# The spectrum of a filter layer kept in the four column groups of its first stage, with GpSimd and VectorE doing the reordering

## The chip, the cores and the metric

One core of one Trainium2 chip. The time is that of the device for one execution, in microseconds (us), as a median of several executions. Besides the times, each kernel was run once with the hardware profiler, whose page and trace are quoted. In these, PE is TensorE's matmuls, PEld its weight loads, ACT is ScalarE, DVE is VectorE, POOL is GpSimd and SP the engine that issues most loads.

## The reference

Two branches on the same input x (2048 rows of 1024 bf16), mixed by a gate, and the gradient of the whole:

```python
def _A_ref(x, w_r, w_i):                      # spectral branch
    X = rfft2(x.astype(float32))              # 2048 x 513 complex
    X = X * (w_r + 1j * w_i)                  # filters, 2048 x 513 each
    return irfft2(X, s=(S, D)).astype(bfloat16)

def _B_ref(x, w1, b1, w2, b2):                # MLP branch, F = 3584
    h = x @ w1 + b1
    h = where(h > 0, h, 0); h = h * h
    return h @ w2 + b2

g = sigmoid((x * gate_w).sum(-1, keepdims=True))
out = g * _A_ref(x, ...) + (1 - g) * _B_ref(x, ...)
# returned: out, and the gradients of x, w_r, w_i, w1, b1, w2, b2, gate_w for grad_out
```

The spectral branch runs forward (on x) and backward (on the gradient) at once; the filters' gradients are products of the two spectra.

## The kernel before

The transform has three parts. A first stage makes, for each row tile, the column transform in four groups of columns (column number modulo 4) and stores it. A middle stage, 16 values of m, finishes the row transform, multiplies by the filters and goes back. A last stage reloads and inverts the columns. The middle stage runs as a generator interleaved with the weight-gradient products of the MLP (chains of 16 matmuls 128x512, accumulated in a bank pw and copied out as wo), a share of steps of the transform per chain. The framework has a scheduler of its own: within these priorities it fixes the order of instructions on each engine.

Parts that the change touches (cuts are marked):

```python
def transform(m, n, pm, x):                   # middle stage: px, then x
    px = fps.tile([P, 2, H], FP32, ..., tag="ps2", bufs=2)      # H = 512
    for T in range(2):
        mm(px[:, T, :], lhsT=am[:, m, n, :], rhs=pm[:, n, T, :], ...)
    for c in range(2):
        nc.scalar.copy(                       # from groups to natural order
            out=x[lanes[n], c, :, 0:H].rearrange("p t (i g) -> p t g i", g=4),
            in_=px[lanes[c]].rearrange("p t (g i) -> p t g i", g=4))

def grads_of_w(m, x):                         # filter gradients
    # ... t1_, t2_: products of the two spectra, on VectorE
    V(out=gs[:, 0, 0:W1], in0=t1_[:, 0, 0:W1], in1=t1_[:, 1, 0:W1], op=ALU.add)
    V(out=gs[:, 1, 0:W1], in0=t2_[:, 1, 0:W1], in1=t2_[:, 0, 0:W1], op=ALU.subtract)
    nc.scalar.mul(out=gw[:, :, 0:W1], in_=gs[:, :, 0:W1], mul=GS)
    # ... edges halved on VectorE, gw stored

for m in range(NM + 1):                       # NM = 16; yields left out
    # transform(m, 0), transform(m, 1)          px -> x
    # back(m - 1), first half                   pv -> vc
    # products(x, w)                            t1, t2
    # back(m - 1), second half                  pv -> pc, si, store of y
    # joined(m)                                 y
    # grads_of_w(m, x); pm = mirrored(m + 1, ...)   next inputs folded

# last stage
load(0), load(1)                              # r <- y, issued by ScalarE
folded(0)                                     # rf <- r at step 2, on VectorE
for n in range(len(tiles) + 1):
    rows_back(n); yield                       # pki, then rt
    # ... columns_back(n - 1), load(n + 2), folded(n + 1)
```

The tiles px, pv, pki and pui share two buffers in PSUM, the memory that TensorE writes its results to.

## Time and profile before

| | before |
|---|---|
| time, median of 4 runs | 1323.4 us (1322.8 to 1324.7) |
| TensorE busy, of the profiled 1323.3 us | 1259.8 us |
| ScalarE / VectorE / GpSimd busy | 580.0 / 703.5 / 215.8 us |
| granted TensorE clock, mean | 0.991 |

TensorE is the engine that sets the time, so the table is read from its idle time and from the clock it is granted.

### The profile page before, as it was taken

The numbers are of one execution on the slowest core, as the hardware profiler recorded it, in microseconds if no ns is written. First come the engines' busy times: TensorE is split into PE (matmuls) and PEld (weight loads), VectorE is DVE, ScalarE is ACT, GpSimd is POOL, SyncE is SP. The second block draws the span as 40 slices with busy tenths as digits, with TensorE's granted clock in tenths as the row PEclk, the third lists the DMA queues.
The fourth block names the chain that finished last, engine by engine and source line by source line (L and its number), as shares of the span: only waits on it lengthen the run. The fifth ranks groups of instructions, "written<-read, shape, count | busy, mean of one in ns | idle before, by whom it ended". The sixth has DMA issues, their size and how long they took to land. (4 is left out here: it accounts for less than half of the span.)

```text
span 1323.3 us, 18166 instructions
## 1 busy us (share of the span) xinstructions
PE 1259.8 (95%) x6753; PEld 612.4 (46%) x6884; DVE 703.5 (53%) x1602; ACT 580.0 (44%) x793; POOL 215.8 (16%) x376
## 2 busy tenths in 40 slices
PE   9999999999999979999889988999999999899997
PEld 5655544555444433444334443555454544444443
DVE  3454424544552154555454554444667686886663
ACT  4656655666533365776665763444211111111110
POOL 0111111111110112132213233121100001000000
PEclk9999999999999999999999999999999999999999
DMA  9566364463528585886857667995789977646540
GB/s 294 181 183 176 128 177 141 160 175 128 151 97 188 162 176 153 216 237 151 189 137 168 129 151 194 288 248 165 213 214 238 223 187 194 196 146 180 157 131 32
DMA packets 326003, 233.26 MB, mean 176 GB/s; under 512 B 195052, under 2 KB 279178, under 8 KB 325658
## 3 DMA queue, kind: packets, MB, share of 16 engines
q1 hardware_dynamic: 290864, 141.19, 44.2%
q0 software_dynamic: 26144, 82.47, 18.5%
q10 hardware_dynamic: 8906, 8.43, 2.2%
q8 instruction: 54, 0.88, 0.3%
q14 instruction: 35, 0.29, 0.1%
HBM read 106.19 MB, written 81.81 MB: 142 GB/s over the span
## 5 line engine op out<-in xcount | busy, mean ns | idle before, releaser
L655 PE MATMUL ph<-xT,w1g 128*128 128x512 bf16 x864 | 216.9, 379 | 2.7 <-DMA w1g<-in_B_w_dram 1.2
L796 PE MATMUL pw<-dbn,grp 128*128 128x512 bf16 x876 | 204.4, 385 | 11.1 <-ACT wo L800 10.0
L665 PE MATMUL pd<-dbT,w2T 128*128 128x512 bf16 x877 | 209.8, 379 | 1.6 <-DVE dhT L669 0.4
L812 PE MATMUL pw<-grp,res 128*128 128x512 bf16 x872 | 202.4, 383 | 7.6 <-ACT wo L817 6.3
L884 PE MATMUL acc<-w,hblk 128*128 128x512 bf16 x873 | 196.2, 379 | 1.2
L669 DVE SCALAR_TENSOR_TENSOR dhT<-pd,rT 128x512 bf16<-128x512 f32 x112 | 77.4, 691 | 203.0 <-PE pd L665 159.8
L366 ACT CAST x<-px 64x1024 f16<-64x1024 f32 x64 | 156.8, 2451 | 3.2 <-PE px L364 2.5
L796 PEld LDWEIGHTS <-grp 128*128 128x128 bf16 x896 | 88.2, 99 | 118.4 <-issue 18.8
L812 PEld LDWEIGHTS <-res 128*128 128x128 bf16 x896 | 87.0, 99 | 106.5 <-issue 10.4
L665 PEld LDWEIGHTS <-w2T 128*128 128x128 bf16 x896 | 87.0, 98 | 103.5 <-issue 1.2
L884 PEld LDWEIGHTS <-hblk 128*128 128x128 bf16 x896 | 86.5, 98 | 98.2
L657 ACT ACTIVATE rT<-ph,b1col 128x512 bf16<-128x512 f32 x112 | 76.9, 687 | 116.5 <-PE ph L655 112.9
L655 PEld LDWEIGHTS <-w1g 128*128 128x128 bf16 x896 | 84.5, 98 | 90.5 <-DMA w1g<-in_B_w_dram 1.5
L950 ACT ACTIVATE g<-gatew_bc,dsc 128x1024 f32<-128x1024 bf16 x16 | 18.3, 1148 | 149.5 <-DVE gxo L993 123.3
L513 ACT CAST rt<-pki 128x1024 f16<-128x1024 f32 x32 | 32.4, 1014 | 102.3 <-PE pki L511 94.0
L658 ACT ACTIVATE h2T<-rT 128x512 bf16<-128x512 bf16 x112 | 70.6, 630 | 2.5
L817 ACT CAST wo<-pw 128x512 bf16<-128x512 f32 x56 | 32.3, 584 | 84.8 <-issue 47.7
L984 PEld LDWEIGHTS <-dS 128*128 128x128 f16 x448 | 43.9, 98 | 52.8
L800 ACT CAST wo<-pw 128x512 bf16<-128x512 f32 x56 | 31.9, 583 | 54.4 <-PE pw L796 26.9
L984 PEld LDWEIGHTS <-hblk 128*128 128x128 bf16 x336 | 32.7, 98 | 43.9 <-DMA hblk<-dhT_scr 3.7
L984 PE MATMUL xX<-dT,dS 128*128 128x512 f16 x224 | 51.0, 379 | 0.0
L283 POOL DMA_DIRECT2D z_scr<-u x32 | 22.8, 714 | 171.5 <-ACT u L278 101.6
(186 smaller groups left out, 1491.8 us busy)
## 6 DMA issues: line engine op xcount, KB each, us to landing
h2T_scr<-h2T POOLq DMA_DIRECT2D x28, 512.0 KB, 4.2
dhT_scr<-dhT POOLq DMA_DIRECT2D x28, 512.0 KB, 4.5
hblk<-h2T_scr SPq DMA_DIRECT2D x8, 1792.0 KB, 8.9
hblk<-dhT_scr SPq DMA_DIRECT2D x8, 1792.0 KB, 8.9
z_scr<-u POOLq DMA_DIRECT2D x32, 256.0 KB, 3.1
z<-z_scr SPq DMA_DIRECT2D x64, 128.0 KB, 3.4
y_scr<-pc POOLq DMA_DIRECT2D x64, 128.0 KB, 2.8
r<-y_scr ACTq DMA_DIRECT2D x32, 256.0 KB, 4.3
```

The source lines that it names most:

```text
L366: nc.scalar.copy(out=x[lanes[n], c, :, 0:H].rearrange("p t (i g) -> p t g i", g=4), in_=px[lanes[c]].rearrange("p t (g i) -> p t g i", g=4),)
L513: nc.scalar.copy(out=rt[n][:], in_=pk[:])
L655: mm(ph[:], lhsT=w1g[:, dc, fc % 2 * P : (fc % 2 + 1) * P], rhs=xT[:, dc, ss], start=(dc == 0), stop=(dc == DC - 1))
L657: nc.scalar.activation(rT[:], ph[:], ACT.Relu, bias=b1col[:, fc : fc + 1])
L658: nc.scalar.activation(h2T, rT[:], ACT.Square)
L665: mm(pd[:], lhsT=w_[:, ec, fc % FGC * P : (fc % FGC + 1) * P], rhs=dbT[:, ec, ss], start=(ec == 0), stop=(ec == DC - 1),)
L669: return STT(out=dhT, in0=pd[:], scalar=2.0, in1=rT[:], op0=ALU.mult, op1=ALU.mult, accum_out=gb1part[:, fc, sb : sb + 1],)
L796: mm(pw[:], lhsT=cur[:, t, fb_ * P : (fb_ + 1) * P], rhs=dbn[:, t, hf * H : (hf + 1) * H], start=(t == 0), stop=(t == NT - 1),)
L812: mm(pw[:], lhsT=xr[t][:, d_ * P : (d_ + 1) * P], rhs=cur[:, t, :], start=(t == 0), stop=(t == NT - 1),)
L817: nc.scalar.copy(out=wo[:], in_=pw[:])
L884: turn["PE"] = mm(acc[:], lhsT=cur[:, fc, t2 * P : (t2 + 1) * P], rhs=w2[:, fc, cs], start=(fc == 0), stop=(fc == FC - 1))
L984: mm(acc[:], lhsT=lhs[:, fc, :], rhs=rhs[:, fc, :], start=start and fc == 0, stop=fc == KH - 1, skip_group_check=True,)
```

## The change

The copies px to x leave the spectrum in the order in which the first stage made it, four groups of 128 columns, so that ScalarE writes contiguously. Everything that meets the spectrum must follow. The filters are brought into groups by GpSimd, and their gradients back to natural order by VectorE, which also takes over the scaling gw. The constants of the last stage are permuted, and its folding reads whole runs. Two empty steps are put between asking for r and its first use.

```diff
-            w = fb.tile([P, 3, LW], BF16, name="w", tag="w", bufs=2)
+            wn = fb.tile([P, 2, LW], BF16, name="wn", tag="wn", bufs=2)
 ...
+        def by_groups(wn):
+            w = fb.tile([P, 3, LW], BF16, name="w", tag="w", bufs=2)
+            G.tensor_copy(
+                out=w[:, 0:2, 0:H].rearrange("p c (g i) -> p c g i", g=4),
+                in_=wn[:, :, 0:H].rearrange("p c (i g) -> p c g i", g=4),
+            )
+            G.tensor_copy(out=w[:, 0:2, H], in_=wn[:, :, H])
+            G.tensor_scalar(out=w[:, 2, 0:W1], in0=w[:, 1, 0:W1], scalar1=-1.0, ...)
+            return w
 ...
-                nc.scalar.copy(
-                    out=x[lanes[n], c, :, 0:H].rearrange("p t (i g) -> p t g i", g=4),
-                    in_=px[lanes[c]].rearrange("p t (g i) -> p t g i", g=4),
-                )
+                nc.scalar.copy(out=x[lanes[n], c, :, 0:H], in_=px[lanes[c]])
 ...
-            nc.vector.tensor_scalar(out=w[:, 2, 0:W1], in0=w[:, 1, 0:W1], scalar1=-1.0, ...)
 ...
-            V(out=gs[:, 0, 0:W1], in0=t1_[:, 0, 0:W1], in1=t1_[:, 1, 0:W1], op=ALU.add)
-            V(out=gs[:, 1, 0:W1], in0=t2_[:, 1, 0:W1], in1=t2_[:, 0, 0:W1], op=ALU.subtract)
+            for c, (a, b, op) in enumerate(((t1_[:, 0], t1_[:, 1], ALU.add), (t2_[:, 1], t2_[:, 0], ALU.subtract))):
+                grouped = lambda t: t[:, 0:H].rearrange("p (g i) -> p g i", g=4)
+                V(out=gs[:, c, 0:H].rearrange("p (i g) -> p g i", g=4), in0=grouped(a), in1=grouped(b), op=op)
+                V(out=gs[:, c, H:W1], in0=a[:, H:W1], in1=b[:, H:W1], op=op)
-            nc.scalar.mul(out=gw[:, :, 0:W1], in_=gs[:, :, 0:W1], mul=GS)
+            nc.vector.tensor_scalar(out=gw[:, :, 0:W1], in0=gs[:, :, 0:W1], scalar1=GS, ...)
 ...
-            a, b = rv[:, :, 1:Q:2], rv[:, :, H - 1 : Q : -2]
+            a, b = rv[:, :, 1::2, 0 : P // 2], rv[:, :, 3::-2, P - 1 : P // 2 - 1 : -1]
 ...
         load(0), load(1)
+        yield
+        yield
         folded(0)
 ...
-    todo = 1 + 6 * (R1 // 2) + 2 * NT
+    todo = 3 + 6 * (R1 // 2) + 2 * NT
```

## The prediction

> **What bounds the kernel now.** I read the busy table first, then a table of stretches, then who waits for whom, then the order of time inside one stretch.
>
> ```profile
> PE 1259.8 (95%) x6753; PEld 612.4 (46%) x6884; DVE 703.5 (53%) x1602; ACT 580.0 (44%) x793; POOL 215.8 (16%) x376
> ```
>
> TensorE is busy for 1259.8 of 1323.3 us, so only what makes it idle, or run at a lower clock, can be won: 63.5 us of idle time in all. The stretches say where that lies (columns: stretch, length, busy time of PE, PEld, DVE, ACT, POOL, then granted clock, DMA share, GB/s).
>
> ```profile
> 446.00:470.00 24.00, 22.40 (x132) 10.55 (x133) 2.70 (x15) 11.91 (x8) 2.56 (x4) 1.00 0.80 209
> 470.00:820.00 350.00, 313.52 (x1415) 140.55 (x1443) 186.13 (x350) 223.21 (x176) 98.50 (x184) 0.98 0.72 172
> 820.00:832.00 12.00, 7.58 (x36) 3.68 (x36) 1.52 (x4) 2.51 (x3) 1.12 (x2) 0.72 0.88 290
> 832.00:930.00 98.00, 97.37 (x605) 51.83 (x616) 42.46 (x156) 41.90 (x66) 20.49 (x38) 1.00 0.79 225
> 930.00:1140.00 210.00, 208.49 (x1141) 103.10 (x1162) 153.00 (x397) 38.67 (x56) 19.45 (x36) 1.00 0.84 212
> ```
>
> The middle stage of the transform (16 values of m, interleaved with the weight-gradient products) runs from 446 to 820 us and holds 36.5 + 1.6 us of the idle time; the seam to the last stage, 820 to 832, holds 4.4 at a clock of 0.72. After 832 TensorE is full (0.6 idle of 98), so what is won before 832 moves the end by the same amount. ScalarE is the busiest helper, 223 of 350 us. Whom TensorE waits for:
>
> ```profile
> PE pv L404 <- ACT x L366: 19.2, 9, 3.0
> PE pw L796 <- ACT wo L800: 10.0, 8, 1.6
> PE pw L812 <- ACT wo L817: 6.3, 4, 1.6
> PE pki L511 <- DMA r<-y_scr: 4.2, 2, 3.3
> ```
>
> 35.5 us end on ScalarE and 4.2 on the first reload of the last stage. Why ScalarE is late is seen in one period of m:
>
> ```profile
> 599.83 1.02 ACT L409 COPY vc<-pv 128x1024 f32<-128x1024 f32 x1
> 603.86 1.06 ACT L440 ACTIVATE gw<-gs 128x1026 bf16<-128x1026 f16 x1 [3.01 <-DVE gs L438]
> 604.82 1.05 ACT L800 CAST wo<-pw 128x512 bf16<-128x512 f32 x2
> 609.62 4.95 ACT L366 CAST x<-px 64x1024 f16<-64x1024 f32 x2
> 605.44 3.61 PE L796 MATMUL pw<-dbn,grp 128*128 128x512 bf16 x16 [1.54 <-ACT wo L800]
> ```
>
> ScalarE stands 3.01 us at the gradient scaling gw, which waits for VectorE, while a finished product bank pw waits behind it in the same queue; when gw is through, wo is copied and TensorE goes on after 1.54 us. The 19.2 us are the other fault: a pair of x copies holds a PSUM buffer for 4.95 us, and where the interleaving puts two transform steps close together, pv waits up to 3.0 us for it.
>
> **What the Trainium skill says.** (1) "SBUF — State Buffer", "Door 1: The DMA port swizzle": 16-byte cachelines, with at least two hits per line needed for full bandwidth. The x copy writes 2-byte elements 8 bytes apart, two per line, so by this it should be free. The trace disagrees:
>
> ```profile
> L366 ACT CAST x<-px 64x1024 f16<-64x1024 f32 x64 | 156.8, 2451 | 3.2 <-PE px L364 2.5
> L513 ACT CAST rt<-pki 128x1024 f16<-128x1024 f32 x32 | 32.4, 1014 | 102.3 <-PE pki L511 94.0
> ```
>
> The same number of elements per partition, from PSUM to f16, takes 2451 ns scattered and 1014 ns contiguous. (2) "VectorE: DVE Perf Modes", "What auto-detection actually checks": two results a cycle only if every 16-bit tensor has step of plus or minus 1. The trace agrees:
>
> ```profile
> L503 DVE TENSOR_TENSOR rf<-r 128x256 f16<-128x256 f16 x32 | 13.5, 422 | 33.8 <-DMA r<-y_scr 27.5 <-PE pki L511 6.3
> L527 DVE TENSOR_TENSOR ev<-e 128x256 f16<-128x256 f16 x32 | 9.2, 287 | 35.9 <-ACT e L520 35.9
> ```
>
> 256 elements at step 2 take 422 ns, unit step 287. (3) "GPSIMD Engine Reference", "Elementwise — side-by-side cycle accounting": about 1.8 cycles per element at 1.2 GHz, 769 ns for 512. (4) The same page, "Specifications": its SBUF interface is shared with VectorE, with contention against VectorE instructions that have two SBUF inputs or use two ports. The trace of before has no GpSimd arithmetic, so it neither confirms nor denies (3) and (4).
>
> **The change part by part.**
>
> ScalarE. 64 x copies become contiguous: 64 x (2451 - 1014) ns = 92 us less. The gw scaling leaves ScalarE: 16 x 1061 ns = 17 us less. Per value of m that is 6.8 us, of 14.6 busy in a period such as 554 to 575. More important than the sum: a pair of x copies then holds its buffer for 2.0 us, and nothing on ScalarE waits for VectorE in this stage.
>
> VectorE, per m. Negation of w leaves: -0.294. Each gs gets a step of 4 on its output, so one element a cycle: slope from the step-2 row (422 - 154)/256 = 1.05 ns, where 154 is the fixed part left by 690 ns for 1024 and 423 for 512 elements at unit step; 154 + 512 x 1.05 = 0.69 us, plus a one-element operation of 0.16 (as dsc, 159 ns), against 0.423 before: 2 x 0.43 = +0.85. gw scaling comes over: about 0.45 (a 1024-element bf16 scaling by a column takes 481). Sum +1.0 us per m, +16 for the stage; if a scattered write hurts VectorE as it does ScalarE, up to +1.2 more per m. VectorE then has 186 + 16 = 202 us, 221 at worst, in some 305: 66 to 72%.
>
> GpSimd, per m: a 1024-element copy, a one-column copy and a 513-element scaling. Estimate from (3): 1.54 + 0.77 + about 0.3 = 2.6 us, 42 in the stage on top of 98 of 350: 46% of 305. The filters are asked for two values of m ahead, so this lies beside other work.
>
> TensorE's work doesn't change. A period is about five product chains of 3.45 us (16 matmuls of 0.216) plus eight 512-column matmuls and some small ones: 17.6 + 1.7 + 0.2 = 19.5 us. The chain x copy, products, y, pv must fit in it. The steps lie 3.9 us apart (608.89, 612.77, 616.66, 620.55 in the trace), so the second px of m comes 3.9 us into its period and the pv that uses its y 7.8 us into the next: 23.4 us. The work in between is 2.6 us on ScalarE with one wo ahead, then on VectorE 2.6 for t1 and t2, 3.7 for the gradients, 2.4 for pc, 2.8 for y: 14.1 us. Some 9 us remain.
>
> Last stage: the filter gradients aside, two rf operations per tile go to unit step: 64 x 0.133 = 8.5 us of VectorE off the path, worth nothing in time. The two extra yields put about 2/1.19 = 1.7 chains, 5.8 us of products, between asking for r and using it; the share of steps per product rises from 129/110 to 131/110 to pay for it, so the rest of the last stage lies as before.
>
> What it gives, in us:
> - pv waiting for x: 19.2, all.
> - pw waiting for wo: 16.3, all but about 1.
> - lower clock: after waits of about 3 us a product chain took 4.8 to 5.1 us in place of 3.45 (at 490, 513, 690 and 713 us), 4 x 1.45 = 5.8; gone with the waits.
> - the seam: from 822.5 to 834.0 TensorE does one chain and two groups of pki, 3.45 + 0.9 = 4.35 us of work in 11.5: 7.2 lost to the reload (4.2 of it as wait, the rest to waits of weight loads and to the lower clock). 5.8 us of cover hides most: 6.
> Sum 19.2 + 15.3 + 5.8 + 6 = 46. I take off 2 for waits that I can't foresee: 44, so 1323.2 - 44 = 1279 us.
>
> **The rivals.**
> (a) VectorE takes ScalarE's place. For: 66 to 72% busy, and it shares the SBUF interface with GpSimd's copies, while most of its products have two SBUF inputs; 2.6 us of GpSimd per m, were all of it to stop VectorE, would bring it to about 81%. Then pv waits for y, or px for the bank that pc frees. Against: 9 us of slack in the chain. If it were eaten, 0.5 to 1 us per m: 1287 to 1295.
> (b) GpSimd's queue becomes the wait: its copies stand in order with the stores of wo, gw and y. If one waits for filters still in flight, the wo buffers stay full and ScalarE stops. Against: wn and w have two buffers each, and the load no longer waits for the products (that held the DMA queue for 44.4 us in total). If it happens in a few periods: +5 to 10 us.
> (c) Only the gw wait goes and pv still waits, because the scattered write wasn't the cause of the 2451 ns (the 64 partitions, or the shift between partition halves). Then 16.3 us and the seam are won, about 23 with some clock: 1300. Against: the row of 1014 ns differs in partitions and in the write alone, and fewer partitions should not cost more.
> (d) The seam's wait only moves, since the reload waits for the last y stores, which end earlier too: 6 us less gain, 1285.
>
> **Range and chances.** The floor is all of 19.2 + 16.3 + 5.8 + 7.2 = 48.5 plus the 1.6 idle at the start: 1273. Rival (a) or (b) at its middle gives 1290. I say 1271 to 1293. 2% is 1296.8; only (c), or (a) and (d) together at their worst, stay above it. Faster 0.90, within 2% 0.09, slower 0.01.
>
> **What would show it.** Right: x copies at about 1.01 us; no TensorE waits for x, wo under 2 us in sum; granted clock 1.00 throughout 470 to 780; TensorE idle in the middle stage under 5 us; gs near 0.69 us each; r's wait under 1.5. Wrong: x copies above 1.3 us (c); TensorE waiting for VectorE's y, pc or pm (a); ScalarE waiting for stores, or VectorE for w (b); pki still waiting 3 us for r (d); or the gain in this stage coming back as idle time after 832.

## More of the kernel before

Line numbers differ between kernels: L366 of before is L377 after (x copies), L440 is L449 (gw), L437 and L438 are L446 and L447 (gs), L357 is L368 (pm), L503 is L513 (rf), and the pw matmuls are L796 and L812 before, L808 and L824 after.

## The result, and the profile after

The changed kernel takes 1285.4 us (median of 4 runs, 1284.1 to 1286.0) against 1323.4: 38.0 us less. The ratio is 0.971, 95% interval 0.9693 to 0.9727. All ratios here are the mean time of one kernel's runs over that of the other's of the same rounds, so not quite the ratio of the medians quoted beside them. The profiled execution was the fastest of the four and spans 1282.3 us, 41.0 less than that of before. A second profile of the same kernel, taken later, spans 1285.2.

The busy table of the changed kernel:

```profile
PE 1259.7 (98%) x6884; PEld 610.6 (48%) x6884; DVE 737.9 (58%) x1634; ACT 474.1 (37%) x777; POOL 275.7 (22%) x424
```

The two busy totals of TensorE, 1259.8 and 1259.7 us, can't be compared as they stand: the trace of before lacks 131 of its 6884 matmuls. The second profile of the changed kernel (e11) lacks as many and shows 1252.7 us, some 7 less than before. So the 63.5 us of idle time that the prediction starts from are by about as much too many. ScalarE lost 105.9 us, VectorE gained 34.4 and GpSimd 59.9. Now the stretches of the middle stage, before and then after (columns as in the prediction: stretch, length, busy time of PE, PEld, DVE, ACT, POOL, granted clock, DMA share, GB/s):

```profile
480.00:520.00 40.00, 30.87 (x129) 13.21 (x130) 18.60 (x33) 27.00 (x19) 9.31 (x18) 0.91 0.67 171
520.00:740.00 220.00, 200.29 (x909) 90.04 (x926) 115.71 (x220) 144.19 (x110) 58.56 (x110) 0.98 0.77 183
```

```profile
446.00:480.00 34.00, 32.26 (x171) 14.61 (x169) 11.95 (x26) 8.84 (x13) 10.95 (x11) 0.95 0.74 189
480.00:520.00 40.00, 37.60 (x171) 16.33 (x169) 31.04 (x59) 16.89 (x21) 22.55 (x32) 0.96 0.85 213
520.00:740.00 220.00, 220.00 (x1040) 100.03 (x1039) 166.04 (x272) 91.02 (x118) 111.42 (x163) 1.00 0.85 201
740.00:800.00 60.00, 57.10 (x285) 26.41 (x284) 27.34 (x60) 18.38 (x26) 19.25 (x36) 0.97 0.78 211
```

From 520 to 740 us TensorE is busy for 220.00 of 220 us at full clock. That part of the stage can give nothing more. What is left lies at the start of the stage and at the seam to the last stage, as the waits of TensorE after the change say:

```profile
PE pki L521 <- DMA r<-y_scr: 2.9, 1, 2.9
PE px L375 <- DVE pm L368: 2.4, 1, 2.4
PE sp L354 <- DVE ed L350: 1.7, 1, 1.7
```

No wait for x or for wo is left: the 35.5 us of these in the table of before are gone entirely. The order of time shows what the two larger ones cost beyond themselves:

```profile
483.05 0.60 PE L375 MATMUL px<-pm,am 128*128 128x512 f16 x2 [2.40 <-DVE pm L368]
484.57 2.34 PE L808 MATMUL pw<-dbn,grp 128*128 128x512 bf16 x5
...
783.82 0.40 PE L521 MATMUL pki<-ki,r 128*128 128x128 f16 x4 [2.90 <-DMA r<-y_scr]
784.53 5.30 PE L824 MATMUL pw<-grp,res 128*128 128x512 bf16 x16
790.11 3.62 PE L824 MATMUL pw<-grp,res 128*128 128x512 bf16 x16
```

The chain at 784.53 takes 5.30 us for 16 matmuls, the one at 790.11 takes 3.62: after a wait TensorE runs for a while at half its clock. The granted clock of this stretch is 0.50:

```profile
784.66:788.07 3.41, 3.41 (x10) 1.21 (x8) 0.49 (x2) 1.01 (x1) 0.54 (x1) 0.50 1.03 374
```

The Trainium skill has this in "TensorE: Matmul & The Clock Gate", "Part 1: The HAM clock gate": the clock falls to half after an idle window of about 3.4 us. The trace agrees in size (between 446 and 832 us each half-clock stretch of both traces lasts 3.41 us or twice that), but here single waits of 2.4 us (px) and 2.9 us (pki), less than a whole window, were enough. At the start of the stage the same follows twice. Between 469.95 and 480.65 us, after the wait for ed, 41 matmuls take 10.70 us, where 41 x 0.216 plus 0.17 of latency (16 matmuls take 3.62) make 9.02. Between 483.05 and 489.09 us, 19 matmuls take 6.0 us in place of 4.3. That is 3.4 us lost to the clock there, the same as half of two stretches of 3.41 us. Before, four such stretches lay in the stage and 6.83 us at the seam; after, two in the stage and one at the seam.

The rows that answer to those of before:

```profile
L377 ACT CAST x<-px 64x1024 f16<-64x1024 f32 x64 | 64.4, 1007 | 6.9 <-PE px L375 6.2
L446 DVE TENSOR_TENSOR gs<-g 128x512 f16<-128x512 f16 x32 | 40.1, 1304 | 0.0
L331 POOL TENSOR_SCALAR w<-w 128x513 bf16<-128x513 bf16 x16 | 28.5, 1780 | 1.5
L326 POOL COPY w<-wn 128x1024 bf16<-128x1024 bf16 x16 | 24.5, 1532 | 31.0 <-DVE t L385 25.8 <-DMA wn<-in_A_w_i_dram 4.6
L442 DVE TENSOR_TENSOR g<-x 128x1026 f16<-128x1026 f16 x16 | 15.6, 977 | 0.0
```

The x copy is at 1007 ns. The scattered writing is now VectorE's, 1304 ns for 512 elements. And g, which the change doesn't touch, went from 691 to 977 ns.

### The profile page after: what moved, and what is told of

Same layout as the page of the kernel before. It is cut to its first block, busy times and chain, and to the rows that moved or that the text cites. A ratio compares the mean times of both kernels' runs of the same rounds, so it can differ in the third digit from the quotient of the medians.

```text
span 1282.3 us, 18371 instructions
## 1 busy us (share of the span) xinstructions
PE 1259.7 (98%) x6884; PEld 610.6 (48%) x6884; DVE 737.9 (58%) x1634; ACT 474.1 (37%) x777; POOL 275.7 (22%) x424
## 4 chain that ended last, share of the span: by engine, by line
PE 57%; DVE 4%; issue 1%; DMA 0%; ACT 0%; ACTq 0%; DVEq 0%
PE pw L824 15%; PE acc L896 14%; PE pw L808 13%; PE xX L996 7%; PE xV L996 4%; PE xZ L996 1%; PE pui L294 1%; PE pki L521 1%; PE pv L411 1%; PE px L375 1%; DVE dT L991 1%; DMA r<-y_scr 0%; DVE dS L984 0%; DVE af L876 0%; DVE g L963 0%
## 5 line engine op out<-in xcount | busy, mean ns | idle before, releaser
L667 PE MATMUL ph<-xT,w1g 128*128 128x512 bf16 x896 | 221.1, 379 | 1.0 <-DMA w1g<-in_B_w_dram 1.0
L808 PEld LDWEIGHTS <-grp 128*128 128x128 bf16 x896 | 87.4, 99 | 105.9 <-issue 4.8
L896 PEld LDWEIGHTS <-hblk 128*128 128x128 bf16 x896 | 86.2, 98 | 98.0
L962 ACT ACTIVATE g<-gatew_bc,dsc 128x1024 f32<-128x1024 bf16 x16 | 18.3, 1148 | 149.3 <-DVE gxo L1005 123.0
L377 ACT CAST x<-px 64x1024 f16<-64x1024 f32 x64 | 64.4, 1007 | 6.9 <-PE px L375 6.2
L722 POOL DMA_DIRECT2D h2T_scr<-h2T x28 | 19.9, 711 | 183.1 <-ACT h2T L670 167.4
L897 DVE SCALAR_TENSOR_TENSOR ot<-acc,omg,af 128x512 bf16<-128x512 f32 x32 | 24.0, 748 | 52.0 <-PE acc L896 51.9
```

The lines of the kernel that those rows point to most:

```text
L377: nc.scalar.copy(out=x[lanes[n], c, :, 0:H], in_=px[lanes[c]])
L667: mm(ph[:], lhsT=w1g[:, dc, fc % 2 * P : (fc % 2 + 1) * P], rhs=xT[:, dc, ss], start=(dc == 0), stop=(dc == DC - 1))
L808: mm(pw[:], lhsT=cur[:, t, fb_ * P : (fb_ + 1) * P], rhs=dbn[:, t, hf * H : (hf + 1) * H], start=(t == 0), stop=(t == NT - 1),)
L896: turn["PE"] = mm(acc[:], lhsT=cur[:, fc, t2 * P : (t2 + 1) * P], rhs=w2[:, fc, cs], start=(fc == 0), stop=(fc == FC - 1))
```

## The experiments

"Changed" is the changed kernel.

| run | edit | median us (range) | ratio to before (95%) |
|---|---|---|---|
| changed | | 1285.4 (1284.1 to 1286.0) | 0.9710 (0.9693 to 0.9727) |
| e1 | before, gw on VectorE | 1311.0 (1310.1 to 1311.0) | 0.9893 (0.9878 to 0.9907) |
| e2 | before, x contiguous | 1285.8 (1285.5 to 1286.2) | 0.9704 (0.9690 to 0.9719) |
| e3 | changed, gw on ScalarE | 1289.1 (1287.4 to 1291.2) | 0.9730 (0.9714 to 0.9746) |
| e4 | changed, no empty steps | 1288.7 (1285.9 to 1290.4) | 0.9719 (0.9698 to 0.9740) |
| e5 | changed, four empty steps | 1282.9 (1281.4 to 1285.2) | 0.9690 (0.9675 to 0.9704) |
| e6 | changed, filters on VectorE | 1282.2 (1279.9 to 1283.6) | 0.9678 (0.9663 to 0.9693) |
| e7 | changed, gs contiguous | 1283.9 (1282.6 to 1285.8) | 0.9697 (0.9683 to 0.9711) |
| e8 | stride probe | 1357.3, one run | |
| e9 | changed, pm early | 1280.8 (1280.2 to 1282.6) | 0.9665 (0.9649 to 0.9681) |
| e10 | e6, e7, e9, five steps | 1279.0 (1276.4 to 1288.7) | 0.9665 (0.9639 to 0.9691) |
| e11 | changed again | 1286.8 (1283.3 to 1288.0) | 0.9708 (0.9689 to 0.9727) |
| e12 | e10 with four steps | 1285.8 (1280.3 to 1289.3) | 0.9712 (0.9686 to 0.9738) |

The runs e1 to e4 were made together on one chip, as were e5 to e8, and e9 to e11; e12 was made by itself. All except e2 and e8 gave correct results; these two are wrong on purpose.

**Are there two faults on ScalarE, or one?** My theory going in, as in the prediction, was two: the x copies are slow, and gw blocks its queue. The first run takes the second alone away.

```diff
 # e1, in the kernel before
-            nc.scalar.mul(out=gw[:, :, 0:W1], in_=gs[:, :, 0:W1], mul=GS)
+            nc.vector.tensor_scalar(out=gw[:, :, 0:W1], in0=gs[:, :, 0:W1], scalar1=GS, ...)
```

> The kernel before with one line changed: the filter-gradient scaling gw runs on VectorE, x copies stay scattered (2.45 us). Theory (two separate faults on ScalarE): only the waits of TensorE for wo (16.3 us before) go, to under 3; the waits of pv for x (19.2) stay between 14 and 24; time 1323 - 16 = about 1307 (1303 to 1312). Rival (the scattered copy is the only cause, ScalarE is simply too full): no more than the 1.06 us x 16 of busy time shifts, the waits for wo stay over 8, time above 1315.

1311.0 us, 13.7 less than before in these rounds (1324.7). The waits of TensorE:

```profile
PE pv L404 <- ACT x L366: 19.9, 9, 3.0
PE pki L511 <- DMA r<-y_scr: 3.9, 2, 3.0
PE pw L796 <- ACT wo L800: 1.9, 2, 1.1
```

The waits for wo fell from 16.3 to 1.9 us and those for x stayed, as the theory has it. Then the other fault alone:

```diff
 # e2, in the kernel before; filters left in natural order, so out[2] and out[3] (the filter gradients) are wrong
-                nc.scalar.copy(
-                    out=x[lanes[n], c, :, 0:H].rearrange("p t (i g) -> p t g i", g=4),
-                    in_=px[lanes[c]].rearrange("p t (g i) -> p t g i", g=4),
-                )
+                nc.scalar.copy(out=x[lanes[n], c, :, 0:H], in_=px[lanes[c]])
```

> The kernel before with contiguous x copies alone; filters and gradients stay in natural order, so the results of the spectral part are wrong on purpose. Theory: x copies 1.01 us, the waits of pv for x go to under 2 us with the lower clock that followed them (19.2 + 5.8 = 25), but gw still stands on ScalarE waiting for VectorE with wo behind it, so waits for wo stay at 8 to 18 us; time about 1298 (1292 to 1304). Rival (one cause only, the scattered copy): waits for wo go under 3 too and the time is about 1285, that of the changed kernel.

1285.8 us: the rival. This one edit gives as much as the whole change gives, although gw still stands on ScalarE and still waits there (32.1 us for gs and 13.7 for a DMA, in the table of waits, against 49.4 for gs before). The waits for wo fell to 1.2 us all the same. One period of this run shows how:

```profile
602.76 1.06 ACT L437 ACTIVATE gw<-gs 128x1026 bf16<-128x1026 f16 x1 [1.74 <-DVE gs L435]
603.60 3.62 PE L793 MATMUL pw<-dbn,grp 128*128 128x512 bf16 x16
603.73 0.57 ACT L797 CAST wo<-pw 128x512 bf16<-128x512 f32 x1
607.11 7.07 PE L793 MATMUL pw<-dbn,grp 128*128 128x512 bf16 x31
```

gw runs at 602.76, and the wo behind it is done at 604.30, while TensorE is in its next chain (603.60 to 607.1) in the other bank. The bank is needed at 607.11, so nothing waits. In the period of before that the prediction shows, gw ran at 603.86 and two copies of wo were then due at once, with both banks full and TensorE standing. VectorE's work on gs starts when x is there, so late x copies make gw late, and a late gw makes wo late. This is read from two periods and not tested apart from the other reading, that ScalarE, with 92 us less of copies, simply has room to catch up. Either way both of the waits, 19.2 and 16.3 us, hang on the x copies, and the second can also be cut at gw. The gains therefore don't add: 13.7 alone and 38.9 alone, 38 together. That e2 and the changed kernel take the same time is in part a balance: e2 doesn't pay for the regrouping (px waits 1.1 us for pm in place of 2.4, and its stage has no half-clock stretch), but the first two pki wait 4.6 us in place of 2.9. What gw and the steps are worth is therefore read from e3 and e4.

```diff
 # e3, in the changed kernel
-            nc.vector.tensor_scalar(out=gw[:, :, 0:W1], in0=gs[:, :, 0:W1], scalar1=GS, ...)
+            nc.scalar.mul(out=gw[:, :, 0:W1], in_=gs[:, :, 0:W1], mul=GS)
```

> The changed kernel with the gw scaling back on ScalarE. Here gw waits for gs operations that take 1.3 us each in place of 0.42, so it stands longer. Theory: waits of TensorE for wo come back, 10 to 25 us, and pv still does not wait for x; time 1285 + 15 = about 1300 (1294 to 1310). Rival (contiguous copies leave ScalarE enough room to catch up): within 4 us of 1285.

1289.1 us, 3.7 above the changed kernel's median, with overlapping intervals (0.9714 to 0.9746 against 0.9693 to 0.9727). The waits for wo are 1.1 us in sum. This is the rival again: with contiguous copies the move of gw is worth between nothing and about 4 us. My theory of two separate faults is refuted by e2 and e3. What holds is one cause, the slow copies, with two waits behind it.

**The two empty steps at the seam.**

```diff
 # e4 (two steps less; e5: two steps more, todo = 5)
         load(0), load(1)
-        yield
-        yield
         folded(0)
-    todo = 3 + 6 * (R1 // 2) + 2 * NT
+    todo = 1 + 6 * (R1 // 2) + 2 * NT
```

> The changed kernel without the two empty steps between asking for r and using it. In the order of instructions on TensorE as built, 31 product matmuls stand between the last si and the first pki without them and 32 with them, as the scheduler had moved product chains ahead of pki by itself. Theory: the steps cover nothing, the first pki waits 2.5 to 4.5 us either way, time within 3 us of 1285. The prediction's view (the steps hide 6 us): the wait grows by 4 to 6 us and the time is about 1290.

1288.7 us, 3.3 above the changed kernel; the runs range over 4.5 us, so the time alone is unclear. In the profile the first two pki wait 4.8 us in place of 2.9:

```profile
PE pki L521 <- DMA r<-y_scr: 4.8, 2, 3.3
```

The half-clock time behind them is 6.83 us in place of 3.41. So the steps do something, 1.9 us of waiting and 1.7 of clock, but not the 6 that the prediction gave them: it took them for 1.7 product chains of cover. The compiled order says why there was so little. Between the last si and the first pki stand 31 product matmuls without the steps, 31 in the kernel before, and 32 with them. The scheduler had already brought forward two chains to cover the reload; the steps give it one matmul more and a tidier order after it.

> The changed kernel with four empty steps in place of two. As built, 48 product matmuls now stand between the last si and the first pki in place of 32, so 3.45 us more cover. Theory: the wait of pki for r (2.9 us) goes to under 0.5 us, the granted clock stays 1.00 there (1.7 us more), time 1285.4 - 4 = about 1281 (1279 to 1283.5). Rival (the reload is asked for later by the same amount, as its issue stands on ScalarE behind a wo copy): the wait stays at 2 to 3 us, time 1285.

1282.9 us, 2.5 below the changed kernel. The compiled order now has 48 matmuls there, and TensorE's waits are:

```profile
PE px L375 <- DVE pm L368: 4.1, 1, 4.1
PE sp L354 <- DVE ed L350: 1.8, 1, 1.8
PE pki L521 <- DMA r<-y_scr: 0.9, 1, 0.9
```

pki waits 0.9 us in place of 2.9, and the 16 matmuls after it run at full clock again. The wait for pm was 4.1 us in this execution against 2.4 in the first profile of the changed kernel; it varies from run to run (4.0 in e11), which is part of the scatter of 2 to 4 us in all these times. What the scatter leaves to the four steps is about 2 to 4 us.

**Is VectorE near to being the bound, and what does GpSimd's help cost?**

```diff
 # e6, in the changed kernel
-            G.tensor_copy(out=w[:, 0:2, 0:H]...)      # likewise the two others of by_groups
+            nc.vector.tensor_copy(out=w[:, 0:2, 0:H]...)
```

> The changed kernel with the regrouping of the filters on VectorE; GpSimd has no arithmetic. Theory (VectorE is beside the path in this stage): about 1.2 to 2 us more VectorE work per m, less about 0.6 us of blocking by GpSimd; the time stays within 5 us of 1285. Rival (a) of the prediction (VectorE is near to being the bound): TensorE waits for pm, y or pc by over 10 us and the time is above 1295.

1282.2 us, 3.2 below the changed kernel. The intervals only just touch (0.9663 to 0.9693, and 0.9693 to 0.9727), so it isn't slower, and probably a little faster. VectorE's rows and, last, its busy total:

```profile
L442 DVE TENSOR_TENSOR g<-x 128x1026 f16<-128x1026 f16 x16 | 11.1, 691 | 0.0
L326 DVE COPY w<-wn 128x1024 bf16<-128x1024 bf16 x16 | 11.0, 688 | 3.3 <-DMA wn<-in_A_w_i_dram 3.3
```

```profile
PE 1257.1 (98%) x6884; PEld 609.7 (48%) x6884; DVE 737.1 (58%) x1682; ACT 474.3 (37%) x777; POOL 216.4 (17%) x376
```

VectorE does the regrouping in 0.69 us where GpSimd takes 1.53, and all three operations in 1.15 us per m (11.0 + 4.7 + 2.6 = 18.3 us over 16) where GpSimd takes 3.83 (1.53 + 0.52 + 1.78). Yet its busy total is 737.1 us with this work and 737.9 without. So GpSimd's arithmetic had made VectorE's own instructions longer by about what this work adds. Summed by line that is about 12 us: g 4.6 (977 ns in place of 691), y 3.3 (796 in place of 692), the one-element gs 2.0, the edges of gw 1.0 and t 0.9. The three operations come to more than this, 18.3 us, but in the trace they partly overlap with their neighbours on VectorE, so they add less than that to the busy total. The Trainium skill names the cause that fits: "SBUF — State Buffer", "Who interferes with whom", says that a VectorE instruction with two SBUF inputs contends with a GpSimd instruction that reads SBUF. The trace agrees: the operations that grew most have two SBUF inputs, and they are back at their old times without GpSimd. Only some of them were hit: g has a median of 693 ns and a maximum of 1608. Offloading to GpSimd freed nothing here.

```diff
 # e7, in the changed kernel: gs as before the change, and
-            nc.vector.tensor_scalar(out=gw[:, :, 0:W1], in0=gs[:, :, 0:W1], scalar1=GS, ...)
+            nc.vector.tensor_scalar(
+                out=gw[:, :, 0:H].rearrange("p c (i g) -> p c i g", g=4),
+                in0=gs[:, :, 0:H].rearrange("p c (g i) -> p c i g", g=4), scalar1=GS, ...)
```

> The changed kernel with gs left in groups (unit step, 0.42 us as before) and the return to natural order made by the gw scaling, which reads with a long step and writes contiguously. Theory: gs back to about 0.42 us, gw about 1.1 us (one element a cycle) in place of 0.43; VectorE loses about 1.5 us per m, 25 us in all. As VectorE is beside the path except at the start of the stage, where px waits 2.4 us for pm, the time falls by 1 to 4 us. Rival: no change in time at all, pm is held by something else.

1283.9 us, 1.5 below the changed kernel, intervals overlapping: no clear change. The gs operations are at 447 and 550 ns and gw at 1363; VectorE's total falls by 12.2 us, to 725.7, about half of what I expected. The wait of px for pm is still there, 3.8 us. VectorE's load as such is beside the path.

**The start of the stage.** If it isn't VectorE's load, it is its order: for m = 0 all of products, gradients and y come ahead of the folding pm for m = 1.

```diff
 # e9, in the changed kernel
                 nc.vector.tensor_copy(out=x[:, :, :, 0::H], in_=ex[:, m])
+                if m + 1 < NM:
+                    pm = mirrored(m + 1, nxt[0])
 ...
-                    pm, w = mirrored(m + 1, nxt[0]), by_groups(nxt[1])
+                    w = by_groups(nxt[1])
```

> The changed kernel with the folding of the next inputs (pm) put ahead of the products in program order. As built, the second px of the stage now stands after 19 product matmuls in place of 41, so the scheduler no longer places it behind all of VectorE's work for m = 0. Theory (at the start of the stage px waits 2.4 us for pm since VectorE does all of m = 0 first, and the lower clock after that and after the idle of sp costs about 3.7): the wait goes under 0.5 us, the clock recovers; 1285.4 - 3 = about 1282 (1280 to 1284). Rival (only the order of waits changes; pv then waits for y of m = 0): the time stays at 1285.

1280.8 us, five runs within 2.4 us, against 1286.8 for the changed kernel (e11) on the same chip: 6.0 less, with disjoint intervals (0.9649 to 0.9681, and 0.9689 to 0.9727). The stretch and the matmul that had waited:

```profile
480.00:520.00 40.00, 39.79 (x186) 18.03 (x189) 32.81 (x61) 16.96 (x23) 22.86 (x34) 1.00 0.93 219
```

```profile
477.55 0.59 PE L375 MATMUL px<-pm,am 128*128 128x512 f16 x2
```

px no longer waits, and the clock of this stretch is 1.00 in place of 0.96. The gain is above the 2.4 to 4.0 us of the wait because the half-clock time behind it goes too.

> The changed kernel itself once more, on the chip of the two runs above, for a comparison on one chip: 1284 to 1286.5 by every theory, and with it the same waits: pki for r 2.9 us, px for pm 2.4.

This is the run that e9 and e10 are compared with. It came out at 1286.8 us; the waits are 2.9 for pki, as expected, and 4.0 for px, where 2.4 was.

**A measurement of strided writes.**

```diff
 # e8, in the changed kernel: x copies with element step 2 (c = 0) and 8 (c = 1);
 # gs: once written with step 2, once both inputs read with step 4
-                nc.scalar.copy(out=x[lanes[n], c, :, 0:H], in_=px[lanes[c]])
+                nc.scalar.copy(out=x[lanes[n], c, :, 0:H].rearrange("p t (i g) -> p t g i", g=2), ...)   # g=8
```

> A measurement, wrong results on purpose: in the changed kernel the x copies write with an element step of 2 (4 bytes) for the real half and of 8 (16 bytes) for the imaginary half; gs writes with step 2 (4 bytes) once, and reads both inputs with step 4 (8 bytes) and writes contiguously once. If the cost is one of the 16-byte line (two elements per line are enough): 4 bytes as contiguous (1.01 us on ScalarE), 16 bytes above 2.45. If it grows with each narrowing of the hits per line: 4 bytes between 1.01 and 2.45, and 16 bytes well above. If any step costs the same: 2.45 for all. On VectorE, if only writing is slow: the reads with step 4 take 0.69 us (one element a cycle), writing with 4 bytes up to 1.3.

In this order: ScalarE at 16 bytes, at 4 bytes, then VectorE reading at 8 bytes, writing at 4 bytes.

```profile
L383 ACT CAST x<-px 64x1024 f16<-64x1024 f32 x32 | 150.5, 4703 | 0.4
L378 ACT CAST x<-px 64x1024 f16<-64x1024 f32 x32 | 41.7, 1304 | 6.4 <-PE px L375 6.0
...
L457 DVE TENSOR_TENSOR gs<-g 128x512 f16<-128x512 f16 x16 | 13.3, 832 | 0.0
L453 DVE TENSOR_TENSOR gs<-g 128x512 f16<-128x512 f16 x16 | 12.1, 753 | 0.0
```

With the 2451 and 1007 ns known already, ScalarE's copy of 1024 two-byte elements takes 1007, 1304, 2451 and 4703 ns at distances of 2, 4, 8 and 16 bytes. Less 155 ns that don't depend on size (512 elements take 585, 1024 take 1014), that is 0.83, 1.12, 2.24 and 4.44 ns per element: from 4 bytes on it doubles with the distance. In other words it is about 4.45 ns per 16 bytes passed over, however many elements are written in them. VectorE's gs at 8 bytes fits the same figure, (1304 - 154)/512 = 2.25 ns. Of the three cases that I had set out the second holds, the cost grows with each narrowing. The means of VectorE's two new rows, 832 and 753 ns, hold some instructions that GpSimd's arithmetic made longer, so their medians count. Reading at 8 bytes:

```profile
L457 DVE TENSOR_TENSOR gs<-g x16: 669/690/1085, 481.6 to 832.1; 128x512 f16<-128x512 f16 x16
```

These are the least, the median and the most: 690 ns, as I expected for reading with a step. Writing at 4 bytes has a median of 728 ns, (728 - 154)/512 = 1.12 ns per element, as on ScalarE.

**All together.**

```diff
 # e10: the changed kernel with the edits of e6, e7 and e9, and five empty steps (todo = 6); e12: four (todo = 5)
```

> The changed kernel with all that helped or is expected to: filters regrouped on VectorE, gs left in groups and gw read with a long step, pm early, and five empty steps at the seam (64 product matmuls between the last si and the first pki). If the parts add up: 1285.4 - 3 (VectorE not blocked) - 3 (start) - 4.6 (seam) = about 1275 (1273 to 1279), and TensorE idle from 446 to 900 us under 3 us. Rival (each removes the same wait in another way, so that they don't add): 1280 or more.

1279.0 us, 1.8 below e9 by medians, with the same ratio (0.9665), since one of six runs took 1288.7. The parts don't add to 1275. TensorE's first wait in the stage is a new one:

```profile
PE pw L831 <- DMA grp<-dhT_scr: 2.4, 1, 2.4
PE sp L354 <- DVE ed L350: 1.4, 1, 1.4
```

> The run with all parts together, with four empty steps at the seam in place of five. With five, a new wait of 2.4 us for the group of the gradient products appeared (its four transposed loads took 33.7 us from first to last, against 13.4 in the changed kernel), and one run was 10 us longer. Theory (the fifth step moves the loads into each other): with four the wait for the group is gone, pki waits about 1 us for r, time 1276 to 1279. Rival (the loads collide however many steps there are, as the stage before is shorter now): a wait of 2 us or more for the group stays, 1279 to 1282.

1285.8 us, with runs from 1280.3 to 1289.3: the rival as to the wait, and slower than either side expected. The wait for the group of gradient products grew:

```profile
PE pw L830 <- DMA grp<-dhT_scr: 5.7, 1, 5.7
```

Its four transposed loads, and the same four of the changed kernel:

```profile
784.33 34.11 SPq L177 DMA_TRANSPOSE grp<-dhT_scr  x4
```

```profile
793.76 13.39 SPq L177 DMA_TRANSPOSE grp<-dhT_scr  x4
```

From the first issue to the last it takes 34.1 us in place of 13.4, and TensorE comes to it before it is there. Just ahead of these in the same queue go the first loads of w2 (five issues from 772.27 us on). I have not taken these apart, so what slows the transposed loads, the w2 loads or the reloads r, is left open. Of all versions e9 is the one to keep: faster than both kernels, and its runs lie within 2.4 us, where those of e10 and e12 spread over 12.3 and 9.0.

## Why the prediction was right or wrong, point by point

The time, 1285.4 us, lies in the range of 1271 to 1293, and the gain is 38 us where 44 was predicted. That the slow copies keep TensorE waiting was right; one attribution was wrong and two terms were mis-sized.

- **"pv waiting for x: 19.2, all."** Right. The copies took 1.007 us (1.01 predicted), and no such wait is left. TensorE's idle time from 446 to 780 us is 4.1 us, under the 5 that were named.
- **"pw waiting for wo: 16.3, all but about 1."** Right in size. Wrong in its ground: the prediction called the x copies "the other fault", apart from gw. e2 removes these waits without touching gw, and e3 puts gw back without getting them back. The x copies alone were worth as much as the whole change. That the sum came out near in spite of this was luck: the change held both edits, so the 16.3 us were won whichever of the two they hung on.
- **"lower clock: ... 5.8; gone with the waits."** Half right. The four stretches cost half of 4 x 3.41 us, 6.8, and are gone; from 520 to 740 us the clock is 1.00. But 3.4 us came back at the start of the stage, behind waits that the prediction had not seen: px for pm (2.4 us, before 0.4) and sp for ed (1.7, before 0.4).
- **The seam, "5.8 us of cover hides most: 6."** This step failed. For the same 4.35 us of work (two groups of pki and a chain) TensorE took 11.5 us before and 9.2 after (780.92 to 790.11): 2.3 won, not 6. The prediction counted steps of the program as matmuls of cover; the compiled order went from 31 to 32. Its rival (d), 6 us less and 1285, was in size what happened; its ground, that the reload waits for the last y stores, wasn't tested.
- **The sum.** As the two profiles have it: 19.2 + 16.3 of waits gone, 6.8 - 3.4 of clock, 2.3 at the seam, less 2.0 + 1.3 for the new waits at the start: 37.9 us, where 46 less an allowance of 2 was predicted and the medians show 38.0. The two profiled executions differ by 41.0; 3 of these are not placed. Two slips in the working carry nothing: five chains of 3.45 us are 17.25, not 17.6, and the range's lower end of 1271 lies below the floor of 1273 worked out beside it.
- **VectorE.** gs was predicted at 0.69 us, with up to 0.6 more each if scattered writing hurts VectorE too. It took 1.30: the worse case, and the same 2.25 ns per element as ScalarE had paid. The one-element operations took 0.28, where 0.16 was predicted. The total rose by 34.4 us where +16 in the stage and -8.5 in the last one were predicted: the rest is this write (the gs rows rose by 35.4 us in place of 13.6) and the interference, less what overlaps. rf fell from 422 to 288 ns, as predicted. In the middle stage TensorE waited for VectorE only at its start, and there for its order more than its load, as e7 and e9 tell apart. So rival (a) was right about the interference and wrong about its effect.
- **GpSimd.** 2.6 us per m were predicted from the skill's figure, which is its best case; 3.83 measured: the copy was right (1.54 and 1.53), the scaling of 513 elements wrong (0.77, measured 1.78). Rival (b), its queue, did not show: ScalarE's one wait for a store (3.0 us, wo for y_scr; before, 4.0 for gw) held up no matmul.
- **Rival (c)**, that the write pattern is not the cause of the slow copy, fell with the first row of the profile.

## What to carry to other kernels

A slow copy in a strict queue is late twice: what needs it waits, and what stands behind its followers waits as well, so don't add up waits that share a cause. Empty steps in a program are cover only if the compiled order shows them; count the instructions between issue and use there. And before work is moved to GpSimd beside a busy VectorE, take the change in VectorE's busy total as the measure, not the work moved.

## What the Trainium skill lacked or had wrong

- "SBUF — State Buffer", "Door 1: The DMA port swizzle": it asks for at least two hits per 16-byte line for full bandwidth. Writes of 2-byte elements need more: at 8 bytes apart (two per line) ScalarE took 2451 ns and VectorE 2.25 ns per element, at 4 bytes (four per line) ScalarE took 1304 ns against 1007 contiguous. From 4 bytes on the runs fit about 4.45 ns per 16-byte line written, whatever the number of elements in it; contiguous, with eight per line, ScalarE took 0.83 ns per element.
- "GPSIMD Engine Reference", "Elementwise — side-by-side cycle accounting": its best case of 1.8 cycles per element fits the regrouping copy (1532 ns for 1024) but not a bf16 scaling of 513 elements, which took 1780 ns on average and 1503 in the median.
- "SBUF — State Buffer", "Who interferes with whom": it has the contention right, but no size for VectorE instructions with two SBUF inputs. Here 3.83 us of GpSimd arithmetic per m, 16 times, made VectorE's instructions about 12 us longer in sum, and VectorE's busy total is as large with the work on GpSimd (737.9 us) as with it on VectorE (737.1).
- "TensorE: Matmul & The Clock Gate", "Part 1: The HAM clock gate": its idle window of about 3.4 us need not be idle throughout. A single wait of 2.9 us was followed by 16 matmuls in 5.30 us in place of 3.62, and one of 2.4 us by 19 in 6.0 in place of 4.3.
